# Turning three chunks of a layer norm on the way in, with mean and 1/std repeated over partitions by DMA

## The chip, the cores and the metric

The kernel runs on one core of one Trainium2 chip. The metric is the device time of one launch in microseconds, as the median of several runs. One further execution is recorded by the hardware profiler; the lines shown here come from that one. The engines are called PE (TensorE's matmuls), PEld (its weight loads), DVE (VectorE), ACT (ScalarE), POOL (GpSimd) and SP (SyncE, which here only issues transfers).

## The reference

The input `q` has 2048 positions of 448 channels, all in float32. It is normalized, and two branches are added to it:

```python
xn = layernorm(q)                                   # over the 448 channels
kv = (causal conv of k with 4 taps) * v
y  = causal conv of kv with a 2048-tap kernel per channel + kv * ssm_D
out = q + xn * y + mish(xn @ w1 + b1) @ w2          # w1: 448 x 1792, w2: 1792 x 448
```

## The kernel before

The positions are handled in 8 chunks of 256 (`NCHUNK`, `CH`); a chunk is two halves of 128 positions (`jj`). Positions are laid on partitions. The two dense layers make up most of TensorE's work. For float32 accuracy each matrix is split into a high part, which a copy rounds to TensorE's float32r, and the low part that is left over (`split`: ScalarE copies, VectorE subtracts). The products high-high, high-low and low-high are added up in PSUM.

A chunk has 7 pairs of hidden blocks (`NP`). Pair `i` of the 56 takes two *slots*: in slot `2i` come its first-layer matmuls (`g1_mm`, line 457, 22 matmuls), in slot `2i + 1` its Mish on ScalarE and the split of the result (`mish`, lines 465, 74 and 75), and behind that the second-layer matmuls of the pair two before (`g2_mm`, lines 482 to 484). There are 116 slots. The order of instructions on each engine is just the order in which the program issues them; nothing is reordered. Other work is put into slots by two lists: `at(slot, ...)` comes ahead of the slot's own work, `after(slot, ...)` behind it. Small VectorE steps of the layer norm wait in a list, `drip`; `dv()` issues the next of them between other VectorE instructions.

The long convolution is a transform in stages: `f1_mm` and `f1_fold` (slots 0 to 63) bring both inputs to DRAM scratch. Slots 61 to 90 read them back in 8 groups and multiply them: `f2_mm` at line 208, the product `prod` on VectorE at line 241, `i1_mm` at line 251, and evacuations by ScalarE at lines 219, 228 and 259. From slot 92 `e_load` reads the result back, `fold` adds and subtracts its halves on VectorE (lines 290 and 292), `i2_mm` (line 308; slots 98, 102, 106 and 110, two chunks each, chunks 6 and 7 first) finishes the transform, and `gate` multiplies it with the normalized input. In one slot the convolution's matmuls come ahead of the dense layers' own.

The layer norm of chunk `c + 1` is done while chunk `c` runs. `ln_load` brings its rows of `q` with positions on partitions (slot 0 of the chunk's 14). `ln_parts` gives the steps: statistics on VectorE (line 379), `power` for 1/std on GpSimd (line 388), `norm` on GpSimd, for chunks 0 and 7 on VectorE (line 392), and `tail`, which repeats the last 64 channels, so that the fourth block of 128 rows of the contraction carries them twice. Then the chunk is turned so that channels lie on partitions: `ln_T` issues 4 transposes on TensorE for each half (line 407), against an identity, into one of the two PSUM tiles that `g1_mm` also uses. `x_split` copies each half to the high part `XH` on ScalarE (line 419) and subtracts for the low part `XL` on VectorE (line 417). The halves are turned in slots 11 and 12 of the 14. For chunks 5 to 7 (`T_LATE`) the split is held back by `turn()` until ScalarE's evacuations of the same slot are issued; VectorE's other work of the slot comes behind it.

The identity and the first transform's matrix are one constant, `f1id`, loaded by one transfer on ScalarE's queue ahead of the first convolution input.

Of the kernel before, what the change touches and what calls it, by code (L numbers as in the profile page):

```python
# [7 lines left out]
F32 = mybir.dt.float32  # L8
F32R = mybir.dt.float32r
AF = mybir.ActivationFunctionType  # L10
ALU = mybir.AluOpType
# [3 lines left out]
S, D, F = 2048, 448, 1792  # L15
NJ = 16
NF = F // 128
NP = NF // 2
CH = 256
NCHUNK = S // CH  # L20
# [18 lines left out]
def tile_kernel(ctx: ExitStack, tc, q, k, v, sk, hT, sD, w1, b1, w2, c_f1, c_g, c_gi, c_i2, out):  # L39
    nc = tc.nc  # L40
    V = nc.vector

# [3 lines left out]
    cp = pool("consts")  # L46
    wp = pool("weights")
    mp = pool("mlp")
# [19 lines left out]
    w1h = wp.tile([128, 4, F], F32R, name="w1h")  # L68
    w1l = wp.tile([128, 3, F], F32R, name="w1l")
# [13 lines left out]
    def dv(n=1):  # L83
        for _ in range(n):
            if drip:
                drip.pop(0)()
# [4 lines left out]
    def at(slot, fn, *args):  # L91
        plan.setdefault(int(slot), []).append((fn, args))
# [25 lines left out]
    def f1_mm(src, g, key):  # L118
        x = src.pop(g)
        PS[key, g] = ps = [pc(), pc()]  # L120
        for b in range(2):
            for h in range(2):
                for jj in range(2):
                    rg = 32 * (2 * b + h)
                    nc.tensor.matmul(ps[h][64 * jj:64 * jj + 64, b, :D], f1[rg:rg + 32, 0:64], x[rg:rg + 32, jj],  # L125
                                     start=True, stop=True, tile_position=(rg, 64 * jj))

    def f1_fold(g, key):
# [183 lines left out]
    def gate(c):  # L312
        p = PS.pop(("P", c))
        for jj in range(2):
            j = 2 * c + jj
            r = rstd[:, j:j + 1]
            x = (Q if late(c) else QA)[c][:, jj]
            o = t3([128, D], "z") if late(c) else x
            V.scalar_tensor_tensor(o, x, mv[:, j, 0:1], p[:, jj, :D], op0=ALU.subtract, op1=ALU.mult)
# [38 lines left out]
        split(w2h[:, 2 * p:2 * p + 2], w2l[:, 2 * p:2 * p + 2], RW.pop(("2", p)))  # L358


    XS, XN, turned = {}, {}, []

    def ln_load(c, eng=None):
        Q[c] = mp.tile([128, 2, D], F32, name="qt", tag="qt", bufs=3)
# [2 lines left out]
        else:  # L367
            for jj in range(2):
                nc.sync.dma_start(Q[c][:, jj], q[:, jj])

    def ln_parts(c):
        st = mp.tile([128, 2, 6], F32, name="bst", bufs=2)
        ve = mp.tile([128, 2], F32, name="ve", bufs=2)
        xn = mp.tile([128, 2, D + 64], F32, name="xn", tag="xn", bufs=1)
        XN[c] = xn
        eng = nc.gpsimd if 0 < c < NCHUNK - 1 else V

        def stats(jj):
            V.bn_stats(st[:, jj], Q[c][:, jj])

        def aggr(jj):
            V.bn_aggr(mv[:, 2 * c + jj], st[:, jj])

        def eps(a, b):
            V.tensor_scalar(ve[:, a:b], mv[:, 2 * c + a:2 * c + b, 1], EPS, None, op0=ALU.add)  # L385

        def power(a, b):
            nc.gpsimd.tensor_tensor(rstd[:, 2 * c + a:2 * c + b], ve[:, a:b], mhalf[:, a:b], op=ALU.pow)  # L388

        def norm(jj):  # L390
            j = 2 * c + jj
            eng.tensor_scalar(xn[:, jj, :D], Q[c][:, jj], mv[:, j, 0:1], rstd[:, j:j + 1],  # L392
                              op0=ALU.subtract, op1=ALU.mult)

        def tail(a, b):
            eng.tensor_copy(xn[:, a:b, D:], xn[:, a:b, D - 64:D])

        return stats, aggr, eps, power, norm, tail

    def ln_stats(c):  # L400
        stats, aggr, eps, power, norm, tail = ln_parts(c)
        drip.extend([lambda: stats(0), lambda: stats(1), lambda: aggr(0), lambda: aggr(1), lambda: eps(0, 2),
                     lambda: [f(*a) for f, *a in ((power, 0, 2), (norm, 0), (norm, 1), (tail, 0, 2))]])

    def transposes(c, jj, p):
        for kt in range(4):
# [6 lines left out]
    def x_split(c, jj, p, lo):  # L413
        x = p.rearrange("p (a b) -> p a b", a=4)
        h, l = (t[:, :, 128 * jj:128 * jj + 128] for t in XS[c])
        if lo:
            V.tensor_sub(l, x, h)
        else:
            nc.scalar.copy(h, x)  # L419

    def ln_T(c, jj):
        if jj == 0:
            dv(len(drip))
            x_tiles(c)
        p = g1p.tile([128, 2, CH], F32, name="pg1").rearrange("p a b -> p (a b)")
        transposes(c, jj, p)

        def halves():
            for lo in range(2):
                x_split(c, jj, p, lo)  # L430

        turned.append(halves)
        if c < T_LATE:
            turn()

    def turn():
        while turned:
            turned.pop()()


    AHL, P1, P2 = {}, {}, {}
# [54 lines left out]
    def mlp_slot(s):  # L496
        i, half = divmod(s, 2)
        n = len(pairs)
        j = i - G2_LAG
        if half == 0:  # L500
            if i < n:
                c, p = pairs[i]
                if c + 1 < NCHUNK:
                    if p == 0:
                        ln_load(c + 1)
                    if p == (3 if c in (0, 2, NCHUNK - 2) else 2):
                        ln_stats(c + 1)
                    if c == 0:
                        dv(len(drip))
                    if p == NP - 1:  # L510
                        ln_T(c + 1, 1)
                g1_mm(i)
        else:
            if i < n:
                c, p = pairs[i]
                if p == NP - 2 and c + 1 < NCHUNK:
# [86 lines left out]
    nc.gpsimd.tensor_tensor(ve1, one, mhalf, op=ALU.pow)  # L603
    ln_load(0)
    w1_load(0)
    nc.scalar.dma_start(f1id, c_f1)
    h_load(H_HEAD, nc.scalar)
    w1_load(1)
    nc.sync.dma_start(b1t, b1)
# [24 lines left out]
    for s in range(nslots):  # L634
        j = s // 2 - G2_LAG - 1
        if s % 2 == 0 and j >= 0 and pairs[j][1] == NP - 1:
            g2_evac(pairs[j][0])
        for fn, args in plan.pop(s, ()):
            fn(*args)
        mlp_slot(s)  # L640
        fns = plan2.pop(s, ())
        for fn, args in fns:
            if fn in (h2_out, v2_out, i1_out):
                fn(*args)
        turn()
        for fn, args in fns:
            if fn not in (h2_out, v2_out, i1_out):
                fn(*args)
# [4 lines left out]
def _constants():  # L653
    import numpy as np

    w = lambda e: np.exp(-2j * np.pi * (np.asarray(e) % 8192) / 8192.0)

    n1 = np.arange(64)
    k1 = np.arange(64)
    W = w(32 * n1[:, None] * (4 * k1[None, :] - 1))  # L660

    W = W.reshape(32, 2, 64).transpose(1, 0, 2).reshape(64, 64)
    Wo = W.reshape(64, 8, 2, 4).transpose(0, 1, 3, 2)
    f1 = np.stack([Wo.real, Wo.imag], axis=4).reshape(64, 128)
# [18 lines left out]
    return dict(c_f1=c(np.stack([f1, np.eye(128)], axis=1)), c_g=c(G.reshape(128, 8, 4, 2, 32)), c_gi=c(GI.reshape(128, 8, 2, 2, 64)),  # L683
                c_i2=c(i2))


# [25 lines left out]
```

## Time and profile before

| | us |
|---|---|
| median of 3 runs | 369.46 (369.13 to 369.48) |
| the profiled execution | 372.47 |
| its span, from first to last instruction | 370.3 |
| PE busy | 362.4 |
| DVE busy | 262.9 |
| ACT busy | 166.2 |
| POOL busy | 73.8 |

Times inside the profile count from the start of the span. In a row of a timeline stand the start, the length, the engine, the line, the operation, what it writes and reads, and in brackets the idle time of the engine before it and what ended that. In a row of grouped instructions stand count, busy time in us, mean length of one in ns, and the idle time before them. The chain of work that ended last is followed backward from the last instruction; a piece of it lasts until the next piece begins.

### The profile page before, as it was taken

What the parts mean: (1) busy time and instruction counts of PE and PEld (TensorE: products, weight loads), DVE (VectorE), ACT (ScalarE), POOL (GpSimd) and SP (SyncE); (2) the same over time, 40 slices, a digit from 0 to 9 for tenths busy, and PEclk for the clock granted to TensorE, in tenths of its full rate; (3) what the DMA queues carried; (4) which work ended last, traced back from release to release, by engine and by line L of the source; (5) the groups of instructions that cost most, each with busy time, mean ns of one, the idle gap of its engine ahead of it and who ended that gap; (6) DMA issues with size and microseconds to landing.
All of it is one profiled execution on the core that took longest, in us unless ns stands there. A gap on an engine that the chain in (4) does not pass through costs nothing.

```text
span 370.3 us, 7468 instructions
## 1 busy us (share of the span) xinstructions
PE 362.4 (98%) x3128; PEld 294.9 (80%) x3128; DVE 262.9 (71%) x358; ACT 166.2 (45%) x277; POOL 73.8 (20%) x59
## 2 busy tenths in 40 slices
PE   6999999999999999999999999999999999999995
PEld 1888889978888989889878666666666889889885
DVE  3799858899999788897605656656285752897751
ACT  2587553334341542352345555556655433235450
POOL 2105100820228221702006000060000005102020
PEclk9699999999999999999999999999999999999999
DMA  8699996838497239433675689897794385959655
GB/s 297 259 269 347 363 363 149 251 115 290 107 295 245 75 76 243 173 83 92 211 239 181 212 228 255 282 267 216 215 306 120 86 249 207 408 204 292 103 71 127
DMA packets 31442, 79.35 MB, mean 214 GB/s; under 512 B 2865, under 2 KB 18098, under 8 KB 31410
## 3 DMA queue, kind: packets, MB, share of 16 engines
q1 hardware_dynamic: 19826, 44.35, 35.4%
q10 hardware_dynamic: 9248, 22.61, 23.4%
q0 software_dynamic: 2336, 11.93, 11.1%
q8 instruction: 24, 0.39, 0.4%
q14 instruction: 8, 0.07, 0.0%
HBM read 50.44 MB, written 28.44 MB: 213 GB/s over the span
## 4 chain that ended last, share of the span: by engine, by line
PE 78%; DVE 9%; DMA 5%; POOL 4%; issue 3%; ACT 1%; DVEq 0%; POOLq 0%; ACTq 0%; SPq 0%
PE pg L457 31%; PE pg L482 10%; PE pg L484 10%; PE pg L483 10%; PE pc L208 7%; PE pc L251 4%; PE pc L125 3%; PE pg L407 2%; DMA x<-in_hT_dram 2%; DVE x L172 2%; PE pc L308 2%; POOL x L155 2%; POOL xn L392 2%; DMA Dkv<-st 1%; DMA av<-Dkv 1%
## 5 line engine op out<-in xcount | busy, mean ns | idle before, releaser
L465 ACT ACTIVATE a<-pg,b1t 128x256 f32<-128x256 f32 x112 | 47.0, 471 | 112.8 <-PE pg L457 97.4
L457 PE MATMUL pg<-XH,w1h 128*128 128x256 f32 x448 | 92.0, 287 | 0.7 <-ACT XH L419 0.7
L457 PEld LDWEIGHTS pg<-XH,w1h 128*128 128x128 f32 x448 | 70.4, 190 | 18.2 <-issue 15.0
L75 DVE TENSOR_TENSOR acl<-a,ach 128x512 fp32r<-128x512 f32 x56 | 38.8, 694 | 63.2 <-ACT ach L74 62.8
L482 PE MATMUL pg<-w2h,ach 128*128 128x448 f32 x224 | 83.0, 370 | 0.0
L484 PE MATMUL pg<-w2h,acl 128*128 128x448 f32 x224 | 81.4, 363 | 0.0
L483 PE MATMUL pg<-w2l,ach 128*128 128x448 f32 x224 | 81.3, 363 | 0.0
L457 PE MATMUL pg<-XL,w1h 128*128 128x256 f32 x448 | 70.2, 279 | 0.0
L457 PEld LDWEIGHTS pg<-XL,w1h 128*128 128x128 f32 x448 | 60.1, 190 | 0.0
L457 PE MATMUL pg<-XH,w1l 128*128 128x256 f32 x336 | 57.3, 279 | 0.0
L482 PEld LDWEIGHTS pg<-w2h,ach 128*128 128x128 f32 x224 | 42.0, 188 | 11.5 <-issue 9.4
L457 PEld LDWEIGHTS pg<-XH,w1l 128*128 128x128 f32 x336 | 47.4, 190 | 0.0
L483 PEld LDWEIGHTS pg<-w2l,ach 128*128 128x128 f32 x224 | 42.1, 188 | 2.6 <-DVE w2l L75 0.2
L484 PEld LDWEIGHTS pg<-w2h,acl 128*128 128x128 f32 x224 | 42.1, 188 | 2.5
L388 POOL TENSOR_TENSOR rstd<-ve,mhalf 128x2 f32<-128x2 f32 (+1 forms) x9 | 9.0, 1003 | 153.5 <-DVE ve L385 148.3
L74 ACT CAST ach<-a 128x512 fp32r<-128x512 f32 x56 | 34.7, 620 | 1.8
L155 POOL TENSOR_TENSOR x<-kr,skb 128x896 f32<-128x896 f32 x8 | 17.0, 2127 | 80.0 <-DVE x L154 59.1
L392 POOL TENSOR_SCALAR xn<-qt,mv,rstd 128x448 f32<-128x448 f32 x12 | 28.5, 2382 | 0.6
L172 DVE TENSOR_TENSOR x<-x 128x896 f32<-128x896 f32 x24 | 26.5, 1105 | 1.0 <-POOL x L155 0.5
L131 ACT COPY st<-pc 128x896 f32<-128x896 f32 x16 | 14.5, 908 | 14.5 <-PE pc L125 14.5
L132 DVE TENSOR_TENSOR st<-pc,st 128x896 f32<-128x896 f32 x16 | 17.4, 1089 | 3.5 <-ACT st L131 3.1
L419 ACT CAST XH<-pg 128x512 fp32r<-128x512 f32 x16 | 9.4, 590 | 21.8 <-PE pg L407 20.4
(71 smaller groups left out, 397.6 us busy)
## 6 DMA issues: line engine op xcount, KB each, us to landing
Dh<-st ACTq DMA_DIRECT2D x16, 448.0 KB, 6.2
Dkv<-st ACTq DMA_DIRECT2D x16, 448.0 KB, 5.2
ah<-Dh SPq DMA_DIRECT2D x8, 896.0 KB, 7.0
av<-Dkv SPq DMA_DIRECT2D x8, 896.0 KB, 5.6
E<-qe ACTq DMA_DIRECT2D x16, 448.0 KB, 5.4
e<-E POOLq DMA_DIRECT2D x8, 896.0 KB, 7.8
kr<-in_k_dram SPq DMA_DIRECT2D x10, 448.0 KB, 6.3
kr<-in_w_dram SPq DMA_DIRECT2D x7, 512.0 KB, 6.5
```

The lines of the kernel that those rows point to most:

```text
L74: nc.scalar.copy(h, raw)
L75: V.tensor_sub(l, raw, h)
L132: V.tensor_add(st[:, 0], e, st[:, 1])
L155: nc.gpsimd.tensor_mul(o, KR[g - u // 2], skb[:, u:u + 1].to_broadcast([128, 2, D]))
L172: V.tensor_add(KV[g], KV[g], o)
L208: nc.tensor.matmul(p[32 * t:32 * t + 32, r, :D], g[rs, t, c], a[rs, t], start=True, stop=True, tile_position=(64 * r, 32 * t))
L392: eng.tensor_scalar(xn[:, jj, :D], Q[c][:, jj], mv[:, j, 0:1], rstd[:, j:j + 1], op0=ALU.subtract, op1=ALU.mult)
L457: nc.tensor.matmul(ps[:, n], l, r, start=n_ == 0, stop=n_ == len(mm) - 1)
L465: nc.scalar.activation(a[:, n], ps[:, n], AF.Mish, bias=b1t[:, 2 * p + n:2 * p + n + 1])
L482: nc.tensor.matmul(ps, ah[:, n, cs], w2h[:, f], start=f == 0, stop=False)
L483: nc.tensor.matmul(ps, ah[:, n, cs], w2l[:, f], start=False, stop=False)
L484: nc.tensor.matmul(ps, al[:, n, cs], w2h[:, f], start=False, stop=f == NF - 1)
```

## The change

For chunks 5, 6 and 7 (`NT` and up) the input comes in a second time, turned by the host: `qT`, with channels on partitions, the last 64 channels doubled, 512 KB a chunk (`xT_load`). The statistics are computed as before from the rows with positions on partitions, a little earlier (`nt_stats`); 1/std is written beside the mean. GpSimd's queue stores the 256 pairs to DRAM (`nt_store`). SyncE's queue loads them back, each half's 128 pairs repeated over all 128 partitions (`nt_row`). VectorE subtracts the mean and multiplies by 1/std, in place, one half at a time, reading every second element of the repeated row (`nt_norm`). Then one copy on ScalarE and one subtraction on VectorE split the whole chunk (`nt_split`). The transposes, the copies out of PSUM and `turn()` go for these chunks. `NT_AT` gives the slots, counted from the start of the chunk before; `nt_norm` and `nt_split` are issued behind the other work of slots 11 and 12. One of the two rows takes the place of the identity, which is not used after chunk 4, so the identity and the matrix `f1` become two constants with two transfers.

```diff
-T_LATE = 5
+NT = 5
+NT_AT = {"q": -4, "x": 0, "stats": 1, "row": 8, "norm": 11, "split": 12}
...
-    f1id = cp.tile([128, 2, 128], F32, name="f1id")
-    f1, ident = f1id[:, 0], f1id[:, 1]
+    MR = {c: dp.tile([2, CH], F32, name="MR") for c in range(NT, NCHUNK)}
+
+    f1 = cp.tile([128, 64], F32, name="f1")
+    idr = cp.tile([128, CH], F32, name="idr")
+    ident = idr[:, 0:128]
...
+    def rs(c):
+        return rstd[:, 2 * c:2 * c + 2] if c < NT else mv[:, 2 * c:2 * c + 2, 1]
...
+    def xT_load(c):
+        XN[c] = xn_tile()
+        nc.sync.dma_start(XN[c], qT[c])
+
+    def nt_stats(c):
+        stats, aggr, eps, power, norm, tail = ln_parts(c)
+        drip.extend([lambda: stats(0), lambda: stats(1), lambda: aggr(0), lambda: aggr(1),
+                     lambda: (eps(0, 2), power(0, 2), nt_store(c))])
+
+    def nt_store(c):
+        nc.gpsimd.dma_start(MR[c].rearrange("j (p t) -> p j t", t=2), mv[:, 2 * c:2 * c + 2])
+
+    def nt_row(c):
+        ROW[c] = idr, (t3 if sp3 else t2)([128, CH], "row", 1)
+        for jj in range(2):
+            nc.sync.dma_start(ROW[c][jj], MR[c][jj].partition_broadcast(128))
+
+    def nt_norm(c):
+        for jj, row in enumerate(ROW.pop(c)):
+            x = XN[c][:, :, 128 * jj:128 * jj + 128]
+            for t, op in enumerate((ALU.subtract, ALU.mult)):
+                m = row.rearrange("p (a t) -> p t a", t=2)[:, t:t + 1].to_broadcast([128, 4, 128])
+                V.tensor_tensor(x, x, m, op=op)
+                dv()
+
+    def nt_split(c):
+        x_tiles(c)
+        nc.scalar.copy(XS[c][0], XN[c])
+        V.tensor_sub(XS[c][1], XN[c], XS[c][0])
+        dv()
...
-        def halves():
-            for lo in range(2):
-                x_split(c, jj, p, lo)
-
-        turned.append(halves)
-        if c < T_LATE:
-            turn()
...
+        for lo in range(2):
+            x_split(c, jj, p, lo)
...
-                if c + 1 < NCHUNK:
+                if c + 1 < NT:
...
+    for c in range(NT, NCHUNK):
+        b = 2 * NP * (c - 1)
+        at(b + NT_AT["q"], ln_load, c)
+        at(b + NT_AT["x"], xT_load, c)
+        at(b + NT_AT["stats"], nt_stats, c)
+        at(b + NT_AT["stats"] + 2, lambda: dv(len(drip)))
+        at(b + NT_AT["row"], nt_row, c)
+        after(b + NT_AT["norm"], nt_norm, c)
+        after(b + NT_AT["split"], nt_split, c)
...
-    nc.scalar.dma_start(f1id, c_f1)
+    nc.scalar.dma_start(ident, c_id)
+    nc.scalar.dma_start(f1, c_f1)
```

More of the change, by code (lines that the diff above doesn't have):

```diff
@@ L38, in tile_kernel @@
 @with_exitstack
-def tile_kernel(ctx: ExitStack, tc, q, k, v, sk, hT, sD, w1, b1, w2, c_f1, c_g, c_gi, c_i2, out):
+def tile_kernel(ctx: ExitStack, tc, q, qT, k, v, sk, hT, sD, w1, b1, w2, c_f1, c_id, c_g, c_gi, c_i2, out):
     nc = tc.nc
@@ L124, in f1_mm @@
                     rg = 32 * (2 * b + h)
-                    nc.tensor.matmul(ps[h][64 * jj:64 * jj + 64, b, :D], f1[rg:rg + 32, 0:64], x[rg:rg + 32, jj],
+                    nc.tensor.matmul(ps[h][64 * jj:64 * jj + 64, b, :D], f1[rg:rg + 32], x[rg:rg + 32, jj],
                                      start=True, stop=True, tile_position=(rg, 64 * jj))
@@ L315, in gate @@
             j = 2 * c + jj
-            r = rstd[:, j:j + 1]
+            r = rs(c)[:, jj:jj + 1]
             x = (Q if late(c) else QA)[c][:, jj]
@@ L358, in w2_split @@
         split(w2h[:, 2 * p:2 * p + 2], w2l[:, 2 * p:2 * p + 2], RW.pop(("2", p)))
-    XS, XN, turned = {}, {}, []
+    XS, XN = {}, {}
     def ln_load(c, eng=None):
@@ L369, in ln_load, with xn_tile @@
                 nc.sync.dma_start(Q[c][:, jj], q[:, jj])
+    def xn_tile():
+        return mp.tile([128, 4, CH], F32, name="xn", bufs=1)
     def ln_parts(c):
@@ L373, in ln_parts @@
         ve = mp.tile([128, 2], F32, name="ve", bufs=2)
-        xn = mp.tile([128, 2, D + 64], F32, name="xn", tag="xn", bufs=1)
-        XN[c] = xn
+        if c < NT:
+            XN[c] = xn = xn_tile().rearrange("p a b -> p (a b)").rearrange("p (j d) -> p j d", j=2)
         eng = nc.gpsimd if 0 < c < NCHUNK - 1 else V
@@ L387, in power @@
         def power(a, b):
-            nc.gpsimd.tensor_tensor(rstd[:, 2 * c + a:2 * c + b], ve[:, a:b], mhalf[:, a:b], op=ALU.pow)
+            nc.gpsimd.tensor_tensor(rs(c)[:, a:b], ve[:, a:b], mhalf[:, a:b], op=ALU.pow)
         def norm(jj):
             j = 2 * c + jj
-            eng.tensor_scalar(xn[:, jj, :D], Q[c][:, jj], mv[:, j, 0:1], rstd[:, j:j + 1],
+            eng.tensor_scalar(xn[:, jj, :D], Q[c][:, jj], mv[:, j, 0:1], rs(c)[:, jj:jj + 1],
                               op0=ALU.subtract, op1=ALU.mult)
@@ L403, in ln_stats @@
                      lambda: [f(*a) for f, *a in ((power, 0, 2), (norm, 0), (norm, 1), (tail, 0, 2))]])
+    ROW = {}
+    def xT_load(c):
[23 more added lines that the diff above has]
+        dv()
     def transposes(c, jj, p):
@@ L515, in mlp_slot @@
                 c, p = pairs[i]
-                if p == NP - 2 and c + 1 < NCHUNK:
+                if p == NP - 2 and c + 1 < NT:
                     ln_T(c + 1, 0)
@@ L644, in tile_kernel @@
                 fn(*args)
-        turn()
         for fn, args in fns:
@@ L682, in _constants @@
     c = lambda a: np.ascontiguousarray(a, dtype=np.float32)
-    return dict(c_f1=c(np.stack([f1, np.eye(128)], axis=1)), c_g=c(G.reshape(128, 8, 4, 2, 32)), c_gi=c(GI.reshape(128, 8, 2, 2, 64)),
+    return dict(c_f1=c(f1[:, :64]), c_id=c(np.eye(128)), c_g=c(G.reshape(128, 8, 4, 2, 32)), c_gi=c(GI.reshape(128, 8, 2, 2, 64)),
                 c_i2=c(i2))
@@ L693 @@
     lay = lambda x: x.reshape(32, 2, 2, 16, D).transpose(2, 1, 0, 3, 4).reshape(128, NJ, D)
+    rows = np.concatenate([np.arange(D), np.arange(384, D)]).reshape(4, 128)
+    turn = lambda x: x.reshape(128, NCHUNK, 2, D)[..., rows].transpose(1, 4, 3, 2, 0).reshape(NCHUNK, 128, 4, CH)
     kpad = np.pad(a["A_k"][0], ((4, 0), (0, 0)))
     arrs = dict(
-        q=lay(a["A_q"][0]), k=np.concatenate([lay(kpad[:S])[:, :, :][:, :4], lay(a["A_k"][0])], axis=1),
+        q=lay(a["A_q"][0]), qT=turn(lay(a["A_q"][0])), k=np.concatenate([lay(kpad[:S])[:, :, :][:, :4], lay(a["A_k"][0])], axis=1),
         v=lay(a["A_v"][0]), sk=a["A_shift_k"].T, hT=lay(a["A_ssm_k"].T), sD=a["A_ssm_D"][None],
```

3 lines of the change are left out of this document (removed).

## The prediction

> **What bounds the kernel now.** I read the page, then busy time by stretches, then the chain of work that ended last, then each engine's instructions in order of time where the change acts. The page's first line gives the length:
>
> ```profile
> span 370.3 us, 7468 instructions
> ```
>
> The shares of busy time on the page are averages over stages with different limits, so the stretches count. These are the ones that matter (start and end; length; busy time and count of PE, PEld, DVE, ACT, POOL; granted clock, DMA share, GB/s):
>
> ```profile
> 197.30:218.00 20.70, 20.70 (x234) 14.82 (x241) 13.54 (x14) 10.65 (x16) 3.83 (x3) 1.00 0.60 182
> 258.00:280.00 22.00, 22.00 (x258) 15.35 (x250) 12.34 (x14) 12.70 (x19) 0.00 (x0) 1.00 0.80 249
> 305.00:320.00 15.00, 15.00 (x110) 14.09 (x117) 7.37 (x9) 5.46 (x11) 5.34 (x8) 1.00 0.74 280
> 320.00:335.00 15.00, 15.00 (x149) 12.19 (x133) 13.92 (x19) 4.19 (x8) 2.88 (x4) 1.00 0.72 270
> ```
>
> The transposes of chunks 5, 6 and 7 lie in the first three. TensorE has no gap in any of them, at the full clock, so an instruction taken from it there should shorten the stretch. VectorE has 7 to 9 us free in the first two. In the third it is half idle, but in the fourth it works 13.92 of 15.00 us, and chunk 7's new VectorE work comes just ahead of that.
>
> **What goes from TensorE.** Eight transposes for each of three chunks. The chain of work that ended last passes through those of chunk 5 (start, us, what):
>
> ```profile
> 194.68 0.40 PE pg L482
> ...
> 201.46 0.59 PE pg L407 x4
> 202.04 0.21 PE pg L482
> ...
> 206.12 0.59 PE pg L407 x4
> 206.71 2.60 PE pg L457 x22
> ...
> 213.61 1.66 PE pc L208 x32
> 215.28 2.71 PE pg L457 x22
> ```
>
> A group of four takes 0.59 us, but the matmul behind it then takes 0.21, where it takes 0.40 right behind the convolution's matmuls: the first group is worth 0.59 + 0.21 - 0.40 = 0.40 us. Behind the second group the 22 matmuls take 2.60, elsewhere 2.71: 0.59 + 2.60 - 2.71 = 0.48 us. That is 0.88 us a chunk, 110 ns a transpose, and 3 x 0.88 = 2.64 us in all: the ceiling of the gain. GpSimd's normalizing of chunks 5 and 6 and VectorE's of chunk 7 go too; I price them at nothing, since TensorE has no gap behind them. GpSimd gets three small DMA issues instead and has nothing else queued there.
>
> **What comes, and what it costs.** Per chunk: four VectorE operations on 128x512 (subtract and multiply, for two halves), a ScalarE copy of 128x1024 in place of two of 128x512, and one VectorE subtraction of 128x1024 in place of two of 128x512. The nearest rows, from the groups by line and from one line's answer (min/median/max in ns):
>
> ```profile
> L75 DVE TENSOR_TENSOR acl<-a,ach 128x512 fp32r<-128x512 f32 x56 | 38.8, 694 | 63.2 <-ACT ach L74 62.8
> ```
> ```profile
> L340 ACT CAST w1h<-kr 128x1024 fp32r<-128x1024 f32 x6 | 6.3, 1047 | 1.4 <-DMA kr<-in_w_dram 1.4
> ```
> ```profile
> L167 DVE TENSOR_TENSOR x<-kr,skb x16: 605/618/979, 62.5 to 170.1; 128x448 f32<-128x448 f32 x16
> ```
>
> No row shows a VectorE operand that steps over every second element, as the mean and 1/std do in the repeated rows. I take 694 ns for each new operation, by the row with the same elements and two SBUF operands. The lower bound is about that: no two-operand row is faster by the element. The upper is the slowest one, 979 ns for 448 elements, that is 1.12 us for 512. [...]
>
> *Chunk 5.* VectorE and ScalarE in order of time, around the old split:
>
> ```profile
> 203.45 0.69 DVE L417 TENSOR_TENSOR XL<-pg,XH 128x512 fp32r<-128x512 f32 x1 [1.41 <-ACT XH L419]
> ...
> 206.18 1.09 DVE L241 TENSOR_TENSOR yc<-yc,yd 128x896 f32<-128x896 f32 x1
> ```
> ```profile
> 209.35 0.84 ACT L465 ACTIVATE a<-pg,b1t 128x256 f32<-128x256 f32 x2 [0.91 <-PE pg L457]
> ...
> 211.04 1.72 ACT L259 COPY qe<-pc 128x896 f32<-128x896 f32 x2 [0.20 <-DMA g<-in_c_g_dram]
> ```
>
> The new operations stand behind the product that ends at 207.27. With the first old split and its wait gone (0.60 + 1.41), the product ends near 205.3. Four operations, 0.60 from start to start and 0.11 more where one needs the last (the spacings in chunk 7's rows below: 313.64 to 314.24, and 1.12 against 1.01 behind the two halves of a fold), take 2.62: 207.9. The ScalarE copy then ends at 208.95, ahead of the Mish that it delays by half a microsecond (TensorE is ready 0.88 before 209.35). From that Mish's start to the evacuation's is 1.69 with a wait of 0.20, so the evacuation runs from 210.44 to 212.16. Its buffers are wanted by the matmuls of 213.61, now at 212.73. So 0.57 us is spare, and the 0.88 is kept. *Chunk 6* has the same order of work and as much free VectorE time (second stretch): I take the same, 0.88 kept and 0.57 spare.
>
> *Chunk 7.* The old splits were put ahead of the folds; the new operations come behind the fold of chunk 6, and the new split behind the fold of chunk 7. VectorE before, then the two inverse-transform steps on the chain:
>
> ```profile
> 313.64 0.68 DVE L417 TENSOR_TENSOR XL<-pg,XH 128x512 fp32r<-128x512 f32 x1
> 314.24 1.08 DVE L290 TENSOR_TENSOR ex<-e 128x896 f32<-128x896 f32 x1
> 315.36 1.09 DVE L292 TENSOR_TENSOR e<-e 128x896 f32<-128x896 f32 x1
> 316.37 0.68 DVE L417 TENSOR_TENSOR XL<-pg,XH 128x512 fp32r<-128x512 f32 x1
> ...
> 320.79 0.68 DVE L319 SCALAR_TENSOR_TENSOR z<-qt,mv,pc 128x448 f32<-128x448 f32 x1 [1.01 <-PE pc L308]
> ...
> 330.07 1.09 DVE L292 TENSOR_TENSOR e<-e 128x896 f32<-128x896 f32 x1
> ```
> ```profile
> 319.77 1.66 PE pc L308 x32
> ...
> 331.46 1.66 PE pc L308 x32
> ```
>
> After: fold 6 from 313.64, where the old split stood, 2.13 long (314.24 to 316.37): 315.77 (its load had landed by 314.24; were it later than 313.64, up to 0.60 is added). New operations: 318.39. Fold 7, 1.12 + 1.09: 320.60. TensorE wants fold 7 for the second half of the first inverse step, at 319.77 + 0.83 (half of 1.66) - 0.88 = 319.72, and waits 0.88 us: this chunk's gain is given back. Fold 7 frees VectorE at 318.39 + 2.13 = 320.52; the split (twice 0.60) and the next pair's (0.60) follow. The gates start at 322.32, not 320.79, so 1.53 late. VectorE has no gap to make that up before the fold that ends at 331.16, now 332.69. TensorE wants it at 331.46 + 0.83 = 332.29 and waits 0.40 us. The lag can be bounded below by zero, if VectorE were handed something earlier; above it grows one for one with slower operations. I take these values.
>
> *Start.* One constant transfer is now two on ScalarE's queue, ahead of the first convolution input, whose landing the chain waits for (it lands at 1.37 + 7.23 = 8.60, and TensorE starts on it):
>
> ```profile
> 0.94 0.39 ACTq L606 DMA_DIRECT2D f1id<-in_c_f_dram  x1
> 1.37 0.45 ACTq L111 DMA_DIRECT2D x<-in_hT_dram  x1
> ```
> ```profile
> 1.37 7.23 DMA x<-in_hT_dram
> ```
>
> One more issue delays it by up to 0.43 (0.94 to 1.37); the two transfers carry less than the one did, which works the other way. Bounds 0 to 0.43, I take 0.30.
>
> *Transfers.* Statistics are finished by the third slot of the chunk before, the rows are wanted in the eleventh: 8 slots at 370.3 / 116 = 3.2 us, some 25 us. Store and row load run one after the other.
>
> ```profile
> e<-E POOLq DMA_DIRECT2D x8, 896.0 KB, 7.8
> ```
>
> Twice this, the longest median on the page, is 15.6 us, so I price their wait at nothing. SyncE issues the row loads and the transposed chunk; behind them stand the loads of the next convolution groups, asked for three slots (some 10 us) ahead. If the spare were gone, VectorE would stand in front of the rows, and with it every Mish split.
>
> **The sum** on the profiled run: -2.64 + 0.88 + 0.40 + 0.30 = -1.06 us; 372.47 becomes 371.41. That run is 3.01 us above the median of 369.46, and what lies around the span does not change, so the median becomes 368.4.
>
> **Rivals.**
> *All is kept* (0.15): VectorE has no lag in chunk 7 and the start costs nothing: -2.64, 366.8. For it: TensorE is full everywhere. Against: 13.92 of 15.00 us.
> *It cancels* (0.19): each spare is 0.4 us shorter than I read it and the start takes its 0.43: within 0.2% (0.74 us, about what a measurement of this kernel can tell from no change), say 369.3.
> *The stepped rows are slow* (0.23): the new operations take longer, which lands on ScalarE's copy and what is queued behind it. With x the extra of four, the sum is -1.06 + 2(x - 0.57) + x; it passes zero at x = 0.73, where one operation takes 0.88 us. At 1.12 us x is 1.7 and the sum +2.9: 372.4, slower. For it: no row shows such an operand. Against: the rows of two operands lie close together, but for a few.
>
> **How the numbers follow.** The forecast has 0.43, mostly faster by over 0.2%. Faster: 0.58 with the first rival; same 0.19; slower 0.23. The range of 8 in 10 runs from the ceiling of the gain, 366.8, to 371.4, which leaves out the worst of the slow rows.
>
> **What would show it.** No transposes after 165 us. The four operations at 0.69 us each. TensorE without gaps near 205 and 265, and with waits for a fold near 319 and 331. The first convolution input landing at 8.9 instead of 8.60. Wrong would be: operations above 0.88 us, VectorE waiting for a row load, or ScalarE's evacuations holding up TensorE in chunks 5 and 6.

## The result, and the profile after

| | before | after |
|---|---|---|
| median of 4 runs each, us | 369.47 (369.13 to 370.26) | 374.34 (373.43 to 375.16) |
| ratio, 95% interval | | 1.0128 (1.0094 to 1.0162) |
| profiled execution, us | 372.47 | 373.43 |
| its span, us | 370.3 | 371.7 |

The change makes the kernel slower by 1.3%, where the forecast was 1.1 us less. The profiled execution of before that the prediction used started late, as the experiments below show. So the stretches are also held against a second profiled execution of the unchanged kernel (368.91 us, span 366.8).

The page of after, length and busy time by engine:

```profile
span 371.7 us, 7440 instructions
...
PE 361.2 (97%) x3104; PEld 291.1 (78%) x3104; DVE 268.7 (72%) x364; ACT 166.0 (45%) x274; POOL 65.9 (18%) x56
```

The four stretches that the prediction showed, in after, with the same columns:

```profile
197.30:218.00 20.70, 20.70 (x217) 14.79 (x218) 16.01 (x19) 11.54 (x17) 0.00 (x0) 1.00 0.71 223
258.00:280.00 22.00, 22.00 (x253) 14.83 (x252) 16.15 (x19) 12.36 (x17) 0.00 (x0) 1.00 0.91 281
305.00:320.00 15.00, 15.00 (x111) 14.15 (x117) 6.86 (x10) 3.39 (x7) 5.07 (x8) 1.00 0.77 281
320.00:335.00 15.00, 14.91 (x135) 10.90 (x120) 14.62 (x20) 4.87 (x10) 2.19 (x4) 1.00 0.64 255
```

TensorE has no gap around chunks 5 and 6, as forecast; VectorE takes the work (13.54 becomes 16.01, 12.34 becomes 16.15). The new instructions, from after's groups:

```profile
L438 DVE TENSOR_TENSOR xn<-xn,idr 128x512 f32<-128x512 f32 x6 | 4.1, 689 | 0.1
L438 DVE TENSOR_TENSOR xn<-xn,row 128x512 f32<-128x512 f32 x6 | 4.1, 689 | 0.1
L444 DVE TENSOR_TENSOR XL<-xn,XH 128x1024 fp32r<-128x1024 f32 x3 | 3.7, 1221 | 1.1 <-ACT XH L443 1.1
L443 ACT CAST XH<-xn 128x1024 fp32r<-128x1024 f32 x3 | 3.1, 1048 | 7.6 <-DVE xn L438 7.6
```

They cost what was forecast. Where the time went shows when the span is cut at the first matmuls of certain groups, read from each timeline (us):

| from ... to | before, as predicted from | before, again | after |
|---|---|---|---|
| start of the span, first convolution matmul | 8.74 | 5.80 | 9.72 |
| first to last group of the first transform | 168.57 | 167.97 | 168.83 |
| last group, first group on `av` | 15.63 | 15.60 | 16.92 |
| first to last group on `av` (chunks 5 and 6 come in here) | 90.66 | 90.66 | 89.12 |
| last group on `av`, last output addition (chunk 7) | 82.87 | 82.87 | 83.38 |

Against the second execution of before, after loses 3.92 + 0.86 at the start, 1.32 ahead of the first group on `av` and 0.51 at the end, and gains 1.54 around chunks 5 and 6: 5.07 in all. The spans differ by 4.9, the medians by 4.87.

**The start.** TensorE's first rows in the first, then the second execution of before, then in after; first the warm-up matmuls (`warm` in the program), then the convolution's:

```profile
0.93 5.80 PE L599 MATMUL pg<-rstd 128*16 128x448 f32 x8 [0.93 <-DVE one L595]
8.74 1.01 PE L125 MATMUL pc<-x,f1id 32*64 32x448 f32 x16 [2.01 <-DMA x<-in_hT_dram]
```
```profile
0.93 4.80 PE L599 MATMUL pg<-rstd 128*16 128x448 f32 x8 [0.93 <-DVE one L595]
5.80 1.01 PE L125 MATMUL pc<-x,f1id 32*64 32x448 f32 x16
```
```profile
0.93 6.00 PE L641 MATMUL pg<-rstd 128*16 128x448 f32 x8 [0.93 <-DVE one L637]
9.72 1.54 PE L131 MATMUL pc<-x,f 32*64 32x448 f32 x16 [2.78 <-DMA x<-in_hT_dram]
```

In the second execution of before the input is there when the warm-up ends, and TensorE waits for nothing. In the other two it waits 2.01 and 2.78 us. The stretch from 9 to 20 us shows what follows (the column before the last two is the granted clock), in the same order:

```profile
9.00:20.00 11.00, 10.32 (x84) 8.82 (x68) 7.92 (x11) 6.72 (x12) 1.01 (x1) 0.69 0.72 268
```
```profile
9.00:20.00 11.00, 10.35 (x86) 9.01 (x87) 9.66 (x13) 8.80 (x14) 1.02 (x1) 1.00 0.98 335
```
```profile
9.00:20.00 11.00, 9.61 (x84) 7.37 (x84) 7.57 (x11) 6.48 (x10) 1.02 (x1) 0.84 0.64 235
```

After the waits of 2.01 and 2.78 us the clock is below full, 0.69 and 0.84, against 1.00 in the execution without a wait. In after the first 16 matmuls of the convolution take 1.54 us where they take 1.01 in the second execution of before; that is part of the 0.86 us in the second row of the table.

What holds the input up can be read from the DMA packets in the traces. The input's 448 KB come on ScalarE's queue (`q10`) in 128 packets of 3584 bytes. SyncE's queue (`q1`) brings the weights of the dense layers (`kr`, 512 KB, packets of 4096 bytes), issued at 1.63 us; the profile counts both queues against the same 16 DMA engines. The packets, the MB and the share of the engines' time of each queue from 0 to 5 us, in the first execution of before, then in after:

```profile
q1 hardware_dynamic: 304, 0.52, 34.8%
q10 hardware_dynamic: 268, 0.55, 28.1%
```
```profile
q1 hardware_dynamic: 386, 0.86, 49.9%
q10 hardware_dynamic: 284, 0.10, 7.5%
```

In before the input's first packet starts at 3.48 us and the weights' first at 4.60. In after the input's starts at 5.03, behind the two constants, and the weights' at 3.78, so the input comes in among the weights: its last packet starts at 8.86. In the second execution of before the last one starts at 5.16. In the first, all but seven have started by 5.2 us too, and these seven follow up to 7.92, most of them 0.29 us apart.

**The first load of the second transform.** Its matmuls in after, and in the second execution of before, where they have no wait:

```profile
188.40 1.74 PE L214 MATMUL pc<-ah,g 64*32 64x448 f32 x32 [1.22 <-DMA ah<-Dh]
```
```profile
182.33 1.74 PE L208 MATMUL pc<-ah,g 64*32 64x448 f32 x32
```

**Chunk 7.** VectorE in after, around the new operations, and TensorE's part of the two inverse-transform steps, from the chain:

```profile
314.63 1.08 DVE L296 TENSOR_TENSOR ex<-e 128x896 f32<-128x896 f32 x1
315.75 1.09 DVE L298 TENSOR_TENSOR e<-e 128x896 f32<-128x896 f32 x1
316.76 1.42 DVE L438 TENSOR_TENSOR xn<-xn,idr 128x512 f32<-128x512 f32 x2
318.09 1.41 DVE L438 TENSOR_TENSOR xn<-xn,row 128x512 f32<-128x512 f32 x2
319.42 1.08 DVE L296 TENSOR_TENSOR ex<-e 128x896 f32<-128x896 f32 x1
320.54 1.09 DVE L298 TENSOR_TENSOR e<-e 128x896 f32<-128x896 f32 x1
```
```profile
321.68 0.97 PE pc L314 x12
...
332.78 1.86 PE pc L314 x32
```

The order is the one forecast: fold 6, four operations, fold 7. The chain runs through VectorE, and TensorE's second half of the first step starts when fold 7 ends. The second step takes 1.86 where it took 1.66.

### The profile page after: what moved, and what is told of

Read it like the earlier page. It is cut to its first block, busy times and chain, and to the rows that moved or that the text cites. A ratio compares the mean times of both kernels' runs of the same rounds, so it can differ in the third digit from the quotient of the medians.

```text
span 371.7 us, 7440 instructions
## 1 busy us (share of the span) xinstructions
PE 361.2 (97%) x3104; PEld 291.1 (78%) x3104; DVE 268.7 (72%) x364; ACT 166.0 (45%) x274; POOL 65.9 (18%) x56
## 4 chain that ended last, share of the span: by engine, by line
PE 73%; DVE 10%; DMA 6%; POOL 4%; issue 3%; ACT 2%; ACTq 0%; SPq 0%; DVEq 0%; POOLq 0%
PE pg L489 29%; PE pg L514 10%; PE pg L515 9%; PE pg L516 9%; PE pc L214 7%; PE pc L257 4%; PE pc L131 2%; DMA x<-in_hT_dram 2%; DMA Dkv<-st 2%; POOL x L161 2%; PE pc L314 2%; DVE x L178 2%; POOL xn L401 2%; DVE acl L81 1%; DMA av<-Dkv 1%
## 5 line engine op out<-in xcount | busy, mean ns | idle before, releaser
L489 PEld LDWEIGHTS pg<-XH,w1h 128*128 128x128 f32 x448 | 69.6, 188 | 19.7 <-issue 16.5
L397 POOL TENSOR_TENSOR mv<-ve,mhalf 128x2 f32<-128x2 f32 x3 | 2.1, 715 | 114.2 <-DVE ve L394 114.2
L401 POOL TENSOR_SCALAR xn<-qt,mv,rstd 128x448 f32<-128x448 f32 x8 | 20.7, 2590 | 0.4
L131 PE MATMUL pc<-x,f 32*64 32x448 f32 x256 | 16.9, 577 | 2.8 <-DMA x<-in_hT_dram 2.8
```

Source lines behind the costliest of these rows:

```text
L489: nc.tensor.matmul(ps[:, n], l, r, start=n_ == 0, stop=n_ == len(mm) - 1)
```

## The experiments

Each was timed beside runs of the kernel before on the same chip; ratios are to those, with a 95% interval. The kernel before had medians of 369.9 to 370.2 there.

### The start: the two constants

The kernel before, unchanged, profiled a second time.

> The kernel before, unchanged, a second time, as a measure of what executions of one kernel differ by, and for a second trace. Its profiled execution took 372.47 us and its other runs 369.1 to 369.5; in that profile TensorE's granted clock is 0.50 from about 9.7 to 16.2 us. Theory A (the cost of the change is mostly at the start, where the first convolution input lands about 1 us later and TensorE then works longer or more often at half clock): the runs at 369 us are those without the half-clock stretch, and a second profile of this kernel has a span near 367 with a clock of 1.00 between 9 and 20 us, or again near 370 with the same stretch. Theory B (the cost lies in the transfers around 180 to 200 us): the clock at the start is alike in all executions and says nothing.

Measured: median 370.26 (368.40 to 372.29), ratio 0.9987 (0.9956 to 1.0018); span 366.8. This is the second execution of the tables above. The same program has its first matmul at 5.80 in one execution and at 8.74 in another, and with what follows that moves the span by 3.5 us.

Then the kernel before with only the constants parted.

```diff
-    f1id = cp.tile([128, 2, 128], F32, name="f1id")
-    f1, ident = f1id[:, 0], f1id[:, 1]
+    f1 = cp.tile([128, 64], F32, name="f1")
+    idr = cp.tile([128, CH], F32, name="idr")
+    ident = idr[:, 0:128]
...
-    nc.scalar.dma_start(f1id, c_f1)
+    nc.scalar.dma_start(ident, c_id)
+    nc.scalar.dma_start(f1, c_f1)
```

> The kernel before with only the start of the change: two constant transfers on ScalarE's queue in place of one; the transposes stay. Theory A: 2 to 4 us slower than before, 371.5 to 373.5. Theory B: at most 0.5 us slower, 369.5 to 370.

Measured: 373.87 (372.83 to 375.58), ratio 1.0087 (1.0059 to 1.0116). The longest piece at the start of its chain:

```profile
1.84 7.89 DMA x<-in_hT_dram
```

The input lands at 9.73, as in after (9.58). This edit alone, with nothing else of the change, costs 0.87%, 3.2 us (2.2 to 4.3).

Now the other way round: the whole change with one constant and one transfer; the whole tile is overwritten by the first row after chunk 4. (Beside a row tile of its own the one constant does not fit: the pool would take 61.5 KB a partition, and 60.78 are left.)

```diff
-    f1 = cp.tile([128, 64], F32, name="f1")
-    idr = cp.tile([128, CH], F32, name="idr")
-    ident = idr[:, 0:128]
+    f1id = cp.tile([128, 2, 128], F32, name="f1id")
+    f1, ident = f1id[:, 0, 0:64], f1id[:, 1]
+    idr = f1id.rearrange("p a b -> p (a b)")
...
-    nc.scalar.dma_start(ident, c_id)
-    nc.scalar.dma_start(f1, c_f1)
+    nc.scalar.dma_start(f1id, c_f1)
...
```

> The changed kernel with the two constants again in one tile and one transfer, as before the change; the repeated row takes the place of that whole tile. Start theory (one more transfer ahead of the first convolution input makes it land about 1 us later, and TensorE more often starts at half clock; alone it cost 0.9% in the kernel before): 3 to 4 us of the 4.9 come back, so 370 to 371, within 0.3% of before. By the predicted terms of the other chunks (-0.88, -0.88, +0.40) alone it would be 368.9; if the first loads of the second transform are late again by 1.3 us, 370.2. Rival (the constants do not matter once the chunks are turned the new way): 373.5 or more.

Measured: 369.69 (368.38 to 372.57), ratio 0.9970 (0.9938 to 1.0001); span 367.0. First convolution matmul and first matmuls on `ah`:

```profile
5.95 1.01 PE L131 MATMUL pc<-x,f1id 32*64 32x448 f32 x16
...
183.68 1.74 PE L214 MATMUL pc<-ah,g 64*32 64x448 f32 x32 [1.34 <-DMA ah<-Dh]
```

The loss is gone, and the wait for `ah` stays: two separate things.

Is it the number of transfers or their place? Here there are still two, but the identity is issued behind the first input.

```diff
-    nc.scalar.dma_start(ident, c_id)
     nc.scalar.dma_start(f1, c_f1)
     ...
+    nc.scalar.dma_start(ident, c_id)
```

> The changed kernel with its two constant transfers, the identity now issued behind the first convolution input: matrix, input, identity. Start theory, if the place in the queue decides: the input is issued at 1.37 us as before the change, has less ahead of it (32 KB for 128 KB), lands at 5.7 to 8.6 us, and the time is 369 to 371. If the number of small pieces in flight decides instead (the two constants come in pieces of 256 and 512 bytes), the input lands near 9.5 us as in the changed kernel and the time stays at 373 to 374.

Measured: 370.14 (369.44 to 373.58), ratio 1.0004 (0.9977 to 1.0031); span 368.4.

```profile
0.93 6.13 PE L641 MATMUL pg<-rstd 128*16 128x448 f32 x8 [0.93 <-DVE one L637]
7.00 1.01 PE L131 MATMUL pc<-x,f 32*64 32x448 f32 x16
```

The input lands 3.9 us after its issue at 1.37, so at 5.3, and TensorE goes from the warm-up to the convolution without a gap; the warm-up itself is 1.3 us longer than in the second execution of before. The input's first packet starts at 3.32 us, the weights' first at 4.52. So with both constants still parted the cost is gone once the identity stands behind the input: what stands ahead of the first input is what costs.

### The store of the pairs

Without chunk 5's part of the change, first with two constants, then with one.

```diff
-NT = 5
+NT = 6
```

> The changed kernel with the new way for chunks 6 and 7 alone (chunk 5 is turned by TensorE as before). Theory A: within 1 us of the changed kernel: about 374 us plus 0.9 for the eight transposes, since the start is as changed. Theory B: the store and the row loads near 180 to 195 us are gone, the first group of the convolution is not late, and 1.4 us come back less 0.9: 373.8 us; in the trace the first loads of the second transform land as before the change (some 1.4 us less between the first-transform matmuls near 178 us and the second-transform matmuls near 195).

> As the run with one constant transfer, but the new way only for chunks 6 and 7; chunk 5 is turned by TensorE. Theory M (the store of 256 small pairs for chunk 5 near 178 us slows the loads of the second transform that follow it): these loads land as before, the stretch from the last first-transform matmuls to the first second-transform group of kv is 15.5 us as before, not 16.9, and the run is 0.5 us faster or the same as with chunk 5 (1.35 us back, 0.88 us lost). Rival N (that lateness is chance of one execution): 0.9 us slower than with chunk 5, and the other run shows 15.5 us too.

Measured: with two 375.20 (374.57 to 375.91), ratio 1.0112 (1.0072 to 1.0151); with one 371.13 (369.26 to 374.24), ratio 1.0034 (1.0000 to 1.0067). In both the wait for `ah` is gone (last group of the first transform to the first on `ah`: 8.56, as before; 9.85 in after). But chunk 5's gain goes too (90.57 and 90.48 against 89.12), and the tail is longer (84.63 and 84.81 against 83.38). In the kernel with one constant, VectorE, just ahead of chunk 7's new operations:

```profile
315.26 1.09 DVE L296 TENSOR_TENSOR ex<-e 128x896 f32<-128x896 f32 x1 [1.34 <-DMA e<-E]
```

Fold 6 now waits 1.34 us for its load. So the edit took one late load away and brought another, and its time settles nothing; only the stretch ahead of `ah` speaks, against chunk 5's transfers.

Which of them? With one constant, only chunk 5's statistics and so its store were moved four slots later, its rows two.

```diff
+        d = 5 if c == NT else NT_AT["stats"]
-        at(b + NT_AT["stats"], nt_stats, c)
+        at(b + d, nt_stats, c)
...
-        at(b + NT_AT["row"], nt_row, c)
+        at(b + (10 if c == NT else NT_AT["row"]), nt_row, c)
```

> As the run with one constant transfer, but for chunk 5 the statistics come 4 slots later and the row load 2 slots later, so that its store is behind the first loads of the second transform. Theory M: the stretch from the last first-transform matmuls to the first second-transform group of kv is 15.5 us, and the run is about 1.3 us faster than with the early store, near 368.9, if the rows still land ahead of the operations (they are wanted some 10 us after). Rival N: no different from the run with the early store.

Measured: 372.74 (370.74 to 375.56), ratio 1.0071 (1.0038 to 1.0103). The wait for `ah` is gone (8.56). The next load has it instead; the row of the waits, and the chain behind it:

```profile
PE pc L214 <- DMA av<-Dkv: 2.6, 1, 2.6
```
```profile
187.99 6.42 DMA av<-Dkv
...
194.54 2.82 PE pc L214 x32
```

The load of `av` lands 6.42 us after its issue, where it took 4.81 in the first profile of before, and the 32 matmuls take 2.82 instead of 1.74; behind the wait of 2.56 us the granted clock is 0.50:

```profile
196.00:198.00 2.00, 2.00 (x18) 0.67 (x3) 1.09 (x1) 1.41 (x2) 0.00 (x0) 0.50 0.32 112
```

The delay moved with the store. Next, with one constant, the store was written in 128 pieces of 16 bytes instead of 256 of 8. The rows then hold mean and 1/std of positions p and p + 128 side by side, so the new operations read every fourth element.

```diff
-        nc.gpsimd.dma_start(MR[c].rearrange("j (p t) -> p j t", t=2), mv[:, 2 * c:2 * c + 2])
+        nc.gpsimd.dma_start(MR[c], mv[:, 2 * c:2 * c + 2].rearrange("p j t -> p (j t)"))
...
-            nc.sync.dma_start(ROW[c][jj], MR[c][jj].partition_broadcast(128))
+            nc.sync.dma_start(ROW[c][h], MR[c][64 * h:64 * h + 64].rearrange("p x -> (p x)").partition_broadcast(128))
...
-                m = row.rearrange("p (a t) -> p t a", t=2)[:, t:t + 1].to_broadcast([128, 4, 128])
+                m = row.rearrange("q (p j t) -> q t j p", j=2, t=2)[:, t:t + 1].to_broadcast([128, 4, 2, 64])
```

> As the run with one constant transfer, but mean and 1/std of a partition's two positions are stored together: 128 pieces of 16 bytes in place of 256 of 8; the row loads have the same bytes, and VectorE reads every fourth element of a row (16 bytes apart) in place of every second. Theory M by the piece (the store occupies each DMA engine for a time by its count of pieces while the loads of the second transform stand behind it): the stretch from the last first-transform matmuls to the first second-transform group of kv, 17.1 us there and 15.6 before the change, becomes about 16.3, the store lands sooner than in 3.8 us. Rival (a fixed cost of the store, or the row loads): 17.1 as before. [...]

Measured: 370.92 (369.81 to 372.85), ratio 1.0017 (0.9997 to 1.0037). The wait for `ah` is gone (8.56). DMA issues between 168 and 183 us, with KB and the us from issue to landing, in the second execution of before, in after, and here:

```profile
ah<-Dh SPq DMA_DIRECT2D x1, 896.0 KB, 6.3
...
g<-in_c_g_dram SPq DMA_DIRECT2D x1, 128.0 KB, 3.4
```
```profile
ah<-Dh SPq DMA_DIRECT2D x1, 896.0 KB, 7.8
...
g<-in_c_g_dram SPq DMA_DIRECT2D x1, 128.0 KB, 5.9
MR<-mv POOLq DMA_DIRECT2D x1, 2.0 KB, 3.4
```
```profile
ah<-Dh SPq DMA_DIRECT2D x1, 896.0 KB, 6.2
...
g<-in_c_g_dram SPq DMA_DIRECT2D x1, 128.0 KB, 4.3
MR<-mv POOLq DMA_DIRECT2D x1, 2.0 KB, 1.9
```

A store of 2 KB lands after 3.4 us in pieces of 8 bytes and after 1.9 in pieces of 16, and with the former the 896 KB load beside it lands 1.5 us later. But the gain is paid back by the new operations:

```profile
L438 DVE TENSOR_TENSOR xn<-xn,row 128x512 f32<-128x512 f32 x6 | 6.5, 1090 | 0.1
L438 DVE TENSOR_TENSOR xn<-xn,f1id 128x512 f32<-128x512 f32 x6 | 6.5, 1086 | 0.1
```

They take 1.09 us at a step of 16 bytes, 0.69 at 8: four of them 1.6 us more a chunk. The tail grows by 1.55 (84.92 against 83.37 with the 8-byte step), one for one, as the prediction's third rival said. Around chunks 5 and 6 the stretch grows by 1.00 (90.12 against 89.12), where that rival's sum gives 2(1.6 - 0.57) = 2.06: the spare there was larger than it was read.

Does the delay grow with the store? One constant, 8-byte pieces, chunk 5's store issued a second time to memory that nobody reads; then the same with 16-byte pieces.

```diff
+        if c == NT:
+            nc.gpsimd.dma_start(MX.rearrange("j (p t) -> p j t", t=2), mv[:, 2 * c:2 * c + 2])
```

> As the run with one constant transfer, but chunk 5's pairs are stored a second time, right behind the first store, to DRAM that nothing reads. Theory M: the loads of the second transform are held up twice as long: the stretch is 15.6 + 2 x 1.5 = 18.6 us. Rival (the lateness comes from something else that chunk 5 adds there, such as the earlier statistics or the row loads): 17.1 us.

> As the run with 16-byte pieces, but chunk 5's store is issued a second time to DRAM that nothing reads: 256 pieces again, of 16 bytes. If the number of pieces makes the loads late (256 did, 128 did not, though 512 did no more than 256), the stretch is near 17 us; if the size of the piece does (8 bytes against 16), it stays at 15.7.

Measured: twice 8 bytes 368.89 (368.26 to 370.14), ratio 0.9972 (0.9955 to 0.9990), the stretch to `ah` 9.93, with one store 9.97. Twice 16 bytes 371.80 (369.39 to 372.74), ratio 1.0041 (1.0015 to 1.0066), the stretch 8.56. The delay does not grow with the number of stores, and 256 pieces of 16 bytes do not bring it. That is what was expected if something else that chunk 5 adds were the cause; but the run with one store in 16-byte pieces has its statistics and its row loads in the same slots and no delay, so it is not these. That does not make the size of the piece the cause: the issue times and landings let another reading stand. In every kernel with the delay the store was still on its way when the load was issued (after: store 177.33 + 3.4 = 180.7, load 180.43; moved later: 185.06 + 4.0 = 189.1, load 187.99). In both with 16 bytes it had landed (172.36 + 1.9 = 174.3, load 175.36; 175.07 + 1.7 = 176.8, load 177.28).

### Chunk 7, and a version that beats both

With one constant, chunk 7's new operations two slots earlier and its split one: ahead of fold 6.

```diff
-        after(b + NT_AT["norm"], nt_norm, c)
-        after(b + NT_AT["split"], nt_split, c)
+        after(b + (9 if c == NCHUNK - 1 else NT_AT["norm"]), nt_norm, c)
+        after(b + (11 if c == NCHUNK - 1 else NT_AT["split"]), nt_split, c)
```

> As the run with one constant transfer, but for chunk 7 alone the subtraction and multiplication come two slots earlier, where VectorE stands idle for some 4 us, and the split one slot earlier, between the two folds. Theory of the prediction's chunk 7 term (they stand ahead of fold 7, TensorE waits for it near 319 and for a later fold near 331): both waits go and the 0.88 of the transposes is kept, so from the last second-transform group to the end about 82.0 us in place of 83.4; 1.3 us faster than with one constant transfer, 368.4. Rival (the loads of the folds decide): the waits stay, now for a load, and the time is as without it, 369.7.

Measured: 367.25 (366.43 to 368.57), ratio 0.9934 (0.9908 to 0.9960); tail 81.88. VectorE around them, and TensorE's inverse-transform steps in the chain:

```profile
304.73 1.41 DVE L438 TENSOR_TENSOR xn<-xn,f1id 128x512 f32<-128x512 f32 x2
306.06 1.41 DVE L438 TENSOR_TENSOR xn<-xn,row 128x512 f32<-128x512 f32 x2
309.03 0.69 DVE L81 TENSOR_TENSOR acl<-a,ach 128x512 fp32r<-128x512 f32 x1 [1.56 <-ACT ach L80]
309.64 1.08 DVE L296 TENSOR_TENSOR ex<-e 128x896 f32<-128x896 f32 x1
```
```profile
314.78 1.66 PE pc L314 x32
...
326.47 1.66 PE pc L314 x32
```

The operations stand in time that VectorE spent idle. Both steps are back at 1.66, VectorE is off the chain, and the tail is 0.99 below before's 82.87: the worth of eight transposes, kept this time.

Last, on top of that, chunk 5's statistics and store three slots earlier, well ahead of the loads.

```diff
+        d = -2 if c == NT else NT_AT["stats"]
-        at(b + NT_AT["stats"], nt_stats, c)
+        at(b + d, nt_stats, c)
...
```

> As the run with chunk 7's operations earlier, and for chunk 5 the statistics three slots earlier too, so that the store of 8-byte pairs has landed well before the first loads of the second transform are issued. If it is the store in front of these loads that makes them late: the stretch from the last first-transform matmuls to the first second-transform group of kv goes from 16.8 back to 15.6 us and the median from 367.3 to about 366.0. If any early small store costs it, or VectorE's earlier statistics hold up the first transform: 367.3 or more.

Measured: 366.78 (365.97 to 367.77), ratio 0.9914 (0.9882 to 0.9946); span 364.7. The store is issued at 166.94, the load of `ah` at 175.56 lands in 6.2 us, and its stretch is 8.56 with the 8-byte pieces kept. The wait for `ah` is gone. The load behind it still has one, longer than the 0.20 us that it had in the whole change with one constant; its cause was not sought:

```profile
189.90 1.74 PE L214 MATMUL pc<-av,g 64*32 64x448 f32 x32 [0.73 <-DMA av<-Dkv]
```

This version beats the kernel before by 0.86% (0.54 to 1.18) and the change as made by more. Against the kernel one edit earlier the gain, 0.5 us, lies within the runs' spread; it is the stretches that show it.

## Why the prediction was wrong

**What goes from TensorE: right.** 0.88 a chunk kept in chunks 5 and 6 would be 1.76; the stretch got 1.54 shorter, and TensorE has no gap there.

**The new operations: right.** 0.689 us against 0.694; no penalty at the step of 8 bytes. The third rival, slow stepped rows, fell, though its cliff exists one step further (1.09 us at 16 bytes). One reading on the way was wrong, without consequence: the prediction calls 694 ns for 512 elements (1.36 ns each) the fastest by the element, while the product of 896 elements that it shows takes 1.09 us, 1.22 each.

**Chunk 7: right.** +0.40 after giving back 0.88 was forecast, +0.51 measured, by the forecast mechanism (VectorE's lag at fold 7 and again at the last fold); the same operations moved ahead of fold 6 take it away. The order and the times of the operations came out as worked out; the two waits did so less well than their sum. The forecast had the first give back just the 0.88 and the second add 0.40. Counted from the last group on `av`, the first step ends 0.23 later than before (322.65 - 284.59 against 321.43 - 283.60), and the second step adds 0.20. That the sum is off by 0.11 only is in part luck.

**The start: the step that failed most.** The prediction added 0.30, with bounds of 0 to 0.43, for one more issue ahead of the input. The issue was indeed 0.47 later (1.84 instead of 1.37). But parting the constants alone costs 3.2 us (2.2 to 4.3). The upper bound took the price of an issue for the price of a transfer standing in the queue: the input's packets started 1.55 us later (5.03 against 3.48), and behind the weights' instead of ahead of them. What hid the rest was the choice of base: the profiled run of before lay 3.01 us above its median, and the prediction took that for time "around the span" that would not change. It was the late start itself, which only some executions of before have, and it stood in a quoted row: the landing after 7.23 us, with a wait on the chain and a clock of 0.69 behind it. The change makes such a start the rule. A sign of it is the mean granted clock of an execution, 0.991 in the first profiled execution of before and 0.999 in the second: it is 0.995 or less in 16 of the 97 executions of before that were timed beside the experiments, in all 12 with only the constants parted, and in all 4 of after. By the second execution of before, the start costs 3.92 + 0.86.

**Transfers: the second step that failed.** They were priced at nothing, because the rows had 25 us to arrive. They did arrive in time. The question left out was what the small store does to the loads of others: in after the load that TensorE waits for is late by 1.3 us, and the delay goes when the store is moved away from it or written in 16-byte pieces.

**The sum.** +4.78 at the start instead of +0.30, +1.32 for the store instead of 0, the rest within 0.35 of the forecast. The 4.78 sets after against an early start of before; by the medians the parted constants cost 3.2. Beside the later runs before had medians of 369.9 to 370.2, by which the whole loss is nearer 4.2 than 4.9. None of the rivals was this one: all looked at VectorE and the gain, none at the first input's landing. The second rival's sum also does not follow from its condition: a spare of 0.57 that is 0.4 shorter still leaves 0.17, so no gain is lost; for its 369.3 the spare would have to be 0.97 shorter.

**What stays open.** Why, with one constant ahead, the last packets of the input fall behind in some executions: of ten such profiles, six have the first convolution matmul at 5.78 to 6.23 and no packet of the input that starts after 5.2 us, and four have it at 7.87 to 9.14, with five to seven packets that start later. The three with two ahead have it at 9.72 to 9.86; in these the weights' first packet starts ahead of the input's, at 3.6 to 3.8 us against 4.6 to 5.0. That this order is the whole of the loss is read from the packets, not tested: no run moved the weights' load. Whether the store delays the load by its 8-byte pieces or by being under way when the load starts; no run has a 16-byte store that overlaps the load. Why fold 6's load is later when chunk 5 is left out of the change.

## What to carry to other kernels

Where the profiled execution lies well above the median, find the excess in its trace before it is called a constant; here it was a wait on the chain, and the change turned the rarer case into the rule. Price a new transfer by what it stands ahead of and what it is in flight beside, not only by when its own data is wanted: here two constants of 64 and 32 KB in place of one of 128 KB ahead of the first input cost 3.2 us, a 2 KB store 1.3. New work for an engine that is full later goes where that engine is idle now: two slots earlier, the same four operations turned +0.5 into -1.0.

## What the runs showed of the hardware

- The landing of the first input did not follow the bytes ahead of it: behind two transfers of 64 and 32 KB it landed at 9.58 us in after and at 9.73 with only the constants parted, behind one of 128 KB at 5.66 and 8.60 in the two executions of before. With two ahead another queue's load gets ahead: its first packet starts at 3.78 and 3.59 us, the input's at 5.03 and 4.89.
- A 2 KB store in 8-byte pieces took 3.4 to 3.8 us to land where it was issued just ahead of the loads, 4.0 where it was moved four slots later, 5.0 where it was moved three slots earlier and, issued twice, 5.0 for the second; in 16-byte pieces it took 1.9, and the second of two 1.7. The 896 KB load issued while the former was on its way took 7.4 to 8.0 us, beside the latter, already landed, 6.2, and 6.3 in the second execution of before.
- TensorE's granted clock was 0.50 from 196 to 198 us behind a wait of 2.56 us in the middle of the kernel (chunk 5's store moved later), and 0.69 and 0.84 from 9 to 20 us behind waits of 2.01 and 2.78 at the start (the first execution of before, and after). Behind 2.26 at the start of the run with two stores in 16-byte pieces it was not seen to fall: groups of three 128x256 matmuls take 0.50 to 0.51 us there from 11 to 15 us, where one takes 0.84 at 13.13 us in the first execution of before, at a clock of 0.50. Behind 1.34 it was 1.00 (183 to 191 us in the whole change with one constant). So of these four waits of 2 to 3 us three were followed by a lower clock and one was not.
- A VectorE operation of 128x512 in float32 took 0.69 us with a second operand that steps by 8 bytes, the same as the split's subtraction of that size (694 ns), whose operands do not step, and 1.09 at 16 bytes.
